# Attention with an infinite memory beside a Fourier filter: stack pieces in another order, chains of reciprocals a step sooner, last zeros all on GpSimd

## The chip, the cores and the metric

The kernel runs on one core of one Trainium2 chip. The metric is the device time of one execution in microseconds (us), the median of several runs.

## The reference

Two independent parts share the program. Part A is a causal multi-head attention of 32 heads of width 18 over 2048 tokens in four segments of 512, with a compressive memory that is carried from segment to segment; part B is a two-dimensional Fourier filter. Cut to what is computed:

```python
# A: x (1,2048,576), wq, wk, wv, wo (576,576), beta (32)
q, k, v = heads(x@wq), heads(x@wk), heads(x@wv)          # (1,32,4,512,18)
phi = lambda t: where(t > 0, t + 1, exp(t)); g = sigmoid(beta)
M = 0; z = 0
for s in range(4):
    p = softmax(qs @ ks^T * 18**-0.5 + causal_mask)
    a_dot = p @ vs
    a_mem = (phi(qs) @ M) / (phi(qs) @ z + 1e-6)
    outs.append(g * a_mem + (1 - g) * a_dot)
    M = M + phi(ks)^T @ vs;  z = z + sum(phi(ks))
a = merge_heads(outs) @ wo
# B: x (1,2048,576)
b = irfft2(rfft2(x) * (w_r + 1j*w_i))
return concatenate([a, b], axis=-1)
```

## The kernel before

The order of all work is written out by hand: each engine does its instructions in the order in which the program emits them. First come the Fourier part and the projections of part A (to about 357 us). Queries and keys go to DRAM as three bf16 parts each (`qkD`), values with a column of ones as `vD`. The change lies in what follows, `attention`.

**Steps and blocks.** The loop `for t in range(133)` in `attention` does one head of one segment a step: `k=t//4` counts groups of four heads, `hh=t%4` the head in the group, `n=t//8` blocks of eight heads, `g=t//32` segments. In step t the row maxima of head t+10 are found (`s1`), the scores of head t are computed and exponentiated (`s2`), and the products with the values of a group that is 5 to 8 steps older are accumulated (`pv`). TensorE takes them in that order, in pieces that alternate: `s1`, `s2`, `s1`, `s2`, `pv`, background, `s1`, `s2`. At the last head of a group (`hh==3`) the parts of P above the diagonal are set to zero by four instructions (`sel`, L697 to L699): before, on GpSimd, but for the groups k=29 to 31 the one of P0 by a minimum with a tile `cap` on VectorE. `cap` is built by GpSimd in steps 3 and 4 (L945, L946). `mpath` turns the maxima of a group into rows of the stack: VectorE, ScalarE and GpSimd (`mh`, L666 and L667), a transpose on TensorE (L670), a copy on ScalarE (`mts`, L673) and a small DMA on GpSimd's queue (L674).

**Stacks.** `s2` multiplies 108 rows: the 18 dimensions of a head six times, in combinations of the three bf16 parts. `stack_dmas(n,0)` returns the six DMAs that fill Q of block n, `stack_dmas(n,1)` those for K (L625; 144 KB and 18 partitions each). Q has three buffers, K four. `load_v(n)` (L632) loads the values of a block into `vs`, three buffers in turn. Before, at the first step of block n, Q of block n+2, K of block n+3 and `load_v(n+2)` are appended to a list `q`, of which two entries are issued a step, one at the start and one at the end. Q and K of a block are first read by `s1` ten steps ahead of its first head, that is in step 8n-2 for block n. All of these go through SP's queue, which issues in order and has at most eight DMAs on their way, since it uses eight semaphores in turn.

**Results of a block.** `pv_out` (L720) copies the sums to `U`, and five DMAs (`u_dmas`, L725 for the denominators `rD`, L730 for `uD`) store them, through a list `qu` of which two a step are issued.

**Chains of reciprocals.** `recip` loads 32 rows of denominators as `ry`, takes the reciprocal on VectorE (L740), scales it on ScalarE, splits it into three bf16 parts (L742 to L746), stores these (L748) and loads them again as 96 rows (L752). Each `yield` in it is a step; `slack` yields stand ahead of the store, two behind it. `rd` is the chain of the memory's denominators (`den`), `rr` that of the softmax, which starts eight steps into the next segment (`ln`), together with the first loads `ux` of the unscaled results. When it is through, `mixed(g)` is appended to the background list `bg`.

**Background.** `run_bg(1.2)` in the middle of a step and `run_bg(0)` at its end take one unit of the list each time 1.0 has been gathered: one a step, and two in every fifth. `mixed(g)` is a list of such units: `c` for `combine` (a product of TensorE that spreads the reciprocals over the rows, L819, in one bank of PSUM; a product on VectorE, L822 or L824; an addition, L825; a copy `oh` on ScalarE, L814, and a remainder `ol`, L809), `m` for the memory's part (L786 to L793) and `p` for the output projection (L856). Additions and remainders run on GpSimd until step 117, and on VectorE from then on. `pq_load` (L759) loads phi(q) for the memory's part, for the first segment that uses it in steps 16 to 20.

The functions that the diff touches, and what calls them:

Of the kernel before, what the change touches and what calls it, by code (L numbers as in the profile page):

```python
# [5 lines left out]
F32=mybir.dt.float32; F32R=mybir.dt.float32r  # L6
# [383 lines left out]
class ATT:  # L390
# [285 lines left out]
    def s2(s,t):  # L676
# [3 lines left out]
        P=s.P[k]  # L680
# [14 lines left out]
        if hh==3:  # L695
            def sel(x,pat):
                if k<29: nc.gpsimd.affine_select(out=x,in_=x,pattern=pat+[[1,128]],compare_op=OP.is_ge,fill=0.0,base=0,channel_multiplier=-1)  # L697
                elif x.tensor is not P[0].tensor: nc.gpsimd.affine_select(out=x,in_=x,pattern=pat+[[1,128]],compare_op=OP.is_ge,fill=0.0,base=0,channel_multiplier=-1)
                else: nc.vector.tensor_tensor(x,x,s.cap[:,None,:].to_broadcast([128,4,128]),op=OP.min)  # L699
            sel(P[0][:,:,:128],[[0,4]])  # L700
            sel(P[1][:,:,:128],[[0,4]])
            sel(P[1][:,:,384:],[[0,4]])
            sel(P[2][:,:,:128],[[0,4]])
# [17 lines left out]
    def u_dmas(s,n):  # L721
# [9 lines left out]
        return L  # L731
    def recip(s,src,dst,gate,eps,load,slack=0):
        nc=s.nc; tp=s.tp
# [14 lines left out]
        nc.sync.dma_start(bass.AP(tensor=dst.tensor,offset=dst.offset,ap=[[128,128],[32*512,3],[1,128]]),w)  # L748
        yield
        yield  # L750
        r=tp.tile([96,512],BF,name=load,bufs=1) if load!="re" else tp.tile([126,1024],BF,name="re",tag="pq",bufs=5)[:96,:512]
# [9 lines left out]
    def den(s,g,lane):  # L761
# [12 lines left out]
        def chain():  # L774
            yield
            yield
            yield
            yield from s.recip(s.dD[g],s.rdD[g],s.gt,True,"rd",2)
        lane.append(chain())
# [20 lines left out]
    def combine(s,g):  # L800

        nc=s.nc; tp=s.tp; xs=s.ux
        s.oh=[None]*5; s.ol=[None]*5
        eng=lambda: nc.vector if s.now>=117 else nc.gpsimd
        yield
        yield
        def low(u):
            r=126 if u<4 else 72
            eng().tensor_tensor(s.ol[u][:r],s.am[u][:r],s.oh[u][:r].bitcast(F32),op=OP.subtract)  # L809
        for t in range(7):  # L810
            if t>1:
                u=t-2; r=126 if u<4 else 72
                s.oh[u]=tp.tile([126,512],F32R,name="oh",bufs=5); s.ol[u]=tp.tile([126,512],F32R,name="ol",bufs=5)
                nc.scalar.copy(s.oh[u][:r],s.am[u][:r])  # L814
                if s.now<117: low(u)
            if t<5:
# [9 lines left out]
                if t<2: s.later(1,lambda t=t: s.ux_load(g,t+3))  # L826
            if t>1 and s.now>=117: low(t-2)
            yield
# [93 lines left out]
    def attention(s,tp,ps):  # L922
# [18 lines left out]
        lane=[]  # L941
        s.cap=tp.tile([128,128],F32,name="cap",bufs=1)
        for t in range(133):
            k,hh=divmod(t,4); n,qd=divmod(k,2); g=k//8
            if t==3: nc.gpsimd.memset(s.cap,3.0e38)  # L945
            if t==4: nc.gpsimd.affine_select(out=s.cap,in_=s.cap,pattern=[[1,128]],compare_op=OP.is_ge,fill=0.0,base=0,channel_multiplier=-1)  # L946
            if hh==0 and qd==0:
                if 0<n<14: q+=s.stack_dmas(n+2,0)
                if 0<n<13: q+=s.stack_dmas(n+3,1)
                if n+2<16: q.append(lambda n=n: s.load_v(n+2))  # L950
            st=t%32
            if 16<=t<21: s.pq_load(1,t-16)
            if t==34: bg.append(s.den(1,lane))
            if st==8 and g>0:
                def ln(g=g):
                    r=s.recip(s.rD[g-1],s.rrD[g-1],s.g1,False,"rr",2)
                    for i in range(8):
# [11 lines left out]
            b=s.s2(t) if t<128 else iter(())  # L969
            if q: q.pop(0)()  # L970
            if qu: qu.pop(0)()
# [23 lines left out]
            for l in list(lane):  # L995
                try: next(l)
                except StopIteration: lane.remove(l)
            if q: q.pop(0)()
            if qu: qu.pop(0)()
# [138 lines left out]
```

## Time and profile before

| | |
|---|---|
| median of 3 runs | 721.9 us (719.81 to 724.74) |
| the profiled execution | 723.57 us |
| its span, first to last instruction | 721.8 us |
| TensorE busy | 686.8 us, 95% |
| VectorE, ScalarE, GpSimd busy | 543.9, 449.0, 210.3 us |
| moved by DMA | 121.04 MB, 168 GB/s over the span |
| granted TensorE clock, mean | 0.997 |

In the profile, PE is TensorE's matmuls, PEld its weight loads, DVE VectorE, ACT ScalarE, POOL GpSimd and SP the engine that issues most DMAs; L697 is line 697 of the kernel. A group or row names the tiles as out<-in. Rows of the list of waits read: who <- whom, us in total, times, longest. Rows of a timeline read: start in us, length in us, engine, line, operation, tiles, form, count, and in brackets the idle time before it and what ended it. Rows of the chain read: start, length, what. A tile whose name is `x` in them is the stack's first buffer.

### The profile page before, as it was taken

The numbers are of one execution on the slowest core, as the hardware profiler recorded it, in microseconds if no ns is written. First come the engines' busy times: TensorE is split into PE (matmuls) and PEld (weight loads), VectorE is DVE, ScalarE is ACT, GpSimd is POOL, SyncE is SP. The second block draws the span as 40 slices with busy tenths as digits, with TensorE's granted clock in tenths as the row PEclk, the third lists the DMA queues.
The fourth block names the chain that finished last, engine by engine and source line by source line (L and its number), as shares of the span: only waits on it lengthen the run. The fifth ranks groups of instructions, "written<-read, shape, count | busy, mean of one in ns | idle before, by whom it ended". The sixth has DMA issues, their size and how long they took to land.

```text
span 721.8 us, 14187 instructions
## 1 busy us (share of the span) xinstructions
PE 686.8 (95%) x4879; PEld 496.2 (69%) x4879; DVE 543.9 (75%) x1215; ACT 449.0 (62%) x1012; POOL 210.3 (29%) x409
## 2 busy tenths in 40 slices
PE   4999999999999999999999899989999999998997
PEld 4999769879879789999744344434565445653587
DVE  5999989799789698887588778877566875666153
ACT  3657785585685564444488678767556775567631
POOL 2110000100100211565066344444233762427210
PEclk9999999999999999999999999999999999999999
DMA  9876436545373568889637666677556664431331
GB/s 322 268 231 214 144 120 200 178 167 178 135 240 121 159 219 271 202 239 216 186 96 178 163 170 149 174 170 168 141 128 176 166 162 128 124 100 43 97 99 65
DMA packets 83244, 121.04 MB, mean 168 GB/s; under 512 B 11352, under 2 KB 50630, under 8 KB 83036
## 3 DMA queue, kind: packets, MB, share of 16 engines
q1 hardware_dynamic: 76580, 104.11, 50.3%
q0 software_dynamic: 6592, 16.03, 7.8%
q8 instruction: 38, 0.62, 0.4%
q14 instruction: 34, 0.28, 0.1%
HBM read 81.78 MB, written 38.24 MB: 166 GB/s over the span
## 4 chain that ended last, share of the span: by engine, by line
PE 71%; DVE 9%; DMA 8%; ACT 6%; issue 4%; POOL 2%; SPq 0%; DVEq 0%; ACTq 0%
PE pj L464 12%; PE pv L714 10%; PE po L856 7%; PE pjv L464 7%; PE s L641 5%; PE s L649 3%; PE s L684 3%; DMA yb<-yout 3%; PE i L300 3%; PE i L311 3%; PE s L688 2%; DMA Qs<-qkD 2%; PE po L886 2%; PE pn L786 2%; PE c L163 2%
## 5 line engine op out<-in xcount | busy, mean ns | idle before, releaser
L645 DVE CUSTOM_DVE_ANT_0 junk<-s,mask 128x512 bf16<-128x512 f32 (+1 forms) x256 | 141.3, 552 | 58.5 <-PE s L641 53.3
L651 DVE TENSOR_REDUCE mx<-s 128x4 f32<-128x512 f32 x128 | 87.9, 687 | 13.7 <-PE s L650 10.8
L714 PE MATMUL pv<-P,vs 128*32 128x512 f32 (+3 forms) x1024 | 89.1, 444 | 1.1 <-DVE P L699 0.4
L685 ACT ACTIVATE P<-s 128x512 f32<-128x512 f32 x128 | 77.5, 605 | 18.0 <-PE s L684 14.3
L694 ACT ACTIVATE P<-s 128x256 f32<-128x256 f32 x128 | 49.9, 390 | 50.6 <-PE s L693 50.5
L690 ACT ACTIVATE P<-s 128x512 f32<-128x512 f32 x128 | 77.4, 604 | 0.0
L697 POOL TENSOR_SCALAR_AFFINE_SELECT P<-P 128x512 f32<-128x512 f32 x116 | 69.8, 637 | 6.1 <-ACT P L694 3.2
L464 PE MATMUL pj<-x,wqkh 128*128 128x512 f32 x162 | 56.4, 409 | 0.0
L511 POOL MEMSET vt<- 128x32 f32 x16 | 2.4, 161 | 151.8 <-PE pm L521 124.1
L210 DVE TENSOR_TENSOR t<-Z 128x580 f32<-128x580 f32 x64 | 46.2, 757 | 0.1
L210 DVE TENSOR_TENSOR Z<-t 128x580 f32<-128x580 f32 x64 | 45.8, 756 | 0.1
L641 PE MATMUL s<-Ks,Qs 108*128 108x512 bf16 (+1 forms) x128 | 42.2, 330 | 0.0
L142 PE MATMUL f<-ftab,eh 128*128 128x290 f32 (+1 forms) x160 | 31.2, 313 | 9.8 <-ACT eh L126 8.9
L300 PE MATMUL i<-civ,Y 128*128 128x256 f32 (+1 forms) x288 | 37.8, 284 | 0.8 <-DVE T L332 0.8
L714 PEld LDWEIGHTS pv<-P,vs 128*32 128x32 f32 x1024 | 22.3, 108 | 22.6 <-issue 15.4
L311 PE MATMUL i<-itab,T 128*128 128x290 f32 (+1 forms) x224 | 36.4, 311 | 0.2 <-DVE yout L319 0.2
L300 PEld LDWEIGHTS i<-civ,Y 128*128 128x128 f32 (+1 forms) x288 | 35.7, 181 | 1.0 <-DVE T L332 1.0
L464 PEld LDWEIGHTS pj<-x,wqkh 128*128 128x128 f32 x162 | 30.4, 188 | 7.7 <-issue 1.0
L464 PE MATMUL pj<-xh,wqkh 128*128 128x512 f32 x90 | 35.6, 396 | 0.0
L464 PE MATMUL pj<-x,wqkl 128*128 128x512 f32 x90 | 35.5, 395 | 0.0
L464 PE MATMUL pj<-xh,wqkl 128*128 128x512 f32 x90 | 35.5, 394 | 0.0
L650 PE MATMUL s<-tri,idb 128*128 128x256 bf16 x128 | 34.9, 273 | 0.0
(213 smaller groups left out, 1819.6 us busy)
## 6 DMA issues: line engine op xcount, KB each, us to landing
qkD<-sp SPq DMA_DIRECT2D x36, 384.0 KB
Ks<-qkD SPq DMA_DIRECT2D x72, 144.0 KB
x<-qkD SPq DMA_DIRECT2D x60, 144.0 KB
Qs<-qkD SPq DMA_DIRECT2D x60, 144.0 KB
xin<-xb SPq DMA_DIRECT2D x16, 384.0 KB
cfw<-cfw POOLq DMA_DIRECT2D x16, 384.0 KB, 4.3
civ<-civ POOLq DMA_DIRECT2D x16, 384.0 KB, 7.4
vs<-vD SPq DMA_DIRECT2D x16, 330.0 KB
```

The source lines that it names most:

```text
L210: v.tensor_tensor(o,a,b,op=op)
L300: nc.tensor.matmul(p[:m,k],Y[i][:,q,c*128:c*128+m],cc[:,hl,o:o+256],start=n==0,stop=n==5)
L311: nc.tensor.matmul(p,x,t,start=n==0,stop=n==6)
L464: s.nc.tensor.matmul(out,a,b,start=i==0,stop=i==len(L)-1)
L641: nc.tensor.matmul(out,Q[:108,h,128*i:128*i+128],K[:108,h,:128*(i+1)],start=True,stop=True)
L645: nc.vector.tensor_tensor_reduce(out=junk[:,:w],in0=src,in1=s.mask[:,512-w:],scale=1.0,scalar=-3.0e38, op0=OP.add,op1=OP.max,accum_out=s.m ...
L651: nc.vector.tensor_reduce(out=s.mx[k][:,hh],in_=pa.rearrange("p (b c) -> p b c",c=128),axis=mybir.AxisListType.X,op=OP.max)
L685: nc.scalar.activation(P[0][:,hh],p0,AF.Exp,scale=SC)
L690: nc.scalar.activation(P[1][:,hh],p1,AF.Exp,scale=SC)
L697: if k<29: nc.gpsimd.affine_select(out=x,in_=x,pattern=pat+[[1,128]],compare_op=OP.is_ge,fill=0.0,base=0,channel_multiplier=-1)
L714: nc.tensor.matmul(s.pvt[32*hh:32*hh+32,128*j:],vt[:,j,19*h:19*h+32],mv[0][:,hh,mv[1]],start=j==0,stop=j==2,skip_group_check=True)
L856: nc.tensor.matmul(ps,a[t][:r,c],b[:r,t,w],start=i==0,stop=i==14)
```

## The change

Four things are done.

- **Stacks.** In the first step of a block (`r8==0`) the six DMAs of Q are appended, and in this step three entries of `q` are issued at its start and three at its end; in every other step one, at its start. `load_v` is appended a step later, the six DMAs of K another step later. The first segment's `pq_load` moves from steps 16 to 20 to steps 19 to 23.
- **Chains of reciprocals.** `recip` takes the number of yields between its store and its load as `gap`. The chains `rr` and `rd` go from `slack` 2 and two yields to `slack` 1 and three; `rr` starts at the seventh step of a segment and not at the eighth.
- **Zeros.** All four `sel` of every group run on GpSimd; `cap` is gone.
- **Remainders.** The remainders `ol` of the last `combine` run on VectorE from step 110 on, and are held back until step 118 has been passed; its additions stay where they were.

```diff
@@ s2
             def sel(x,pat):
-                if k<29: nc.gpsimd.affine_select(out=x,in_=x,pattern=pat+[[1,128]],compare_op=OP.is_ge,fill=0.0,base=0,channel_multiplier=-1)
-                elif x.tensor is not P[0].tensor: nc.gpsimd.affine_select(out=x,in_=x,pattern=pat+[[1,128]],compare_op=OP.is_ge,fill=0.0,base=0,channel_multiplier=-1)
-                else: nc.vector.tensor_tensor(x,x,s.cap[:,None,:].to_broadcast([128,4,128]),op=OP.min)
+                nc.gpsimd.affine_select(out=x,in_=x,pattern=pat+[[1,128]],compare_op=OP.is_ge,fill=0.0,base=0,channel_multiplier=-1)
@@ recip
-    def recip(s,src,dst,gate,eps,load,slack=0):
+    def recip(s,src,dst,gate,eps,load,slack=0,gap=2):
...
         nc.sync.dma_start(bass.AP(tensor=dst.tensor,offset=dst.offset,ap=[[128,128],[32*512,3],[1,128]]),w)
-        yield
-        yield
+        for _ in range(gap): yield
@@ den
-            yield from s.recip(s.dD[g],s.rdD[g],s.gt,True,"rd",2)
+            yield from s.recip(s.dD[g],s.rdD[g],s.gt,True,"rd",1,3)
@@ combine
-        s.oh=[None]*5; s.ol=[None]*5
+        s.oh=[None]*5; s.ol=[None]*5; lows=[]
         eng=lambda: nc.vector if s.now>=117 else nc.gpsimd
...
-            eng().tensor_tensor(s.ol[u][:r],s.am[u][:r],s.oh[u][:r].bitcast(F32),op=OP.subtract)
+            (nc.vector if s.now>=110 else nc.gpsimd).tensor_tensor(s.ol[u][:r],s.am[u][:r],s.oh[u][:r].bitcast(F32),op=OP.subtract)
...
-                if s.now<117: low(u)
+                if s.now<110: low(u)
...
-            if t>1 and s.now>=117: low(t-2)
+            if t>1 and s.now>=110: lows.append(t-2)
+            if s.now>=118:
+                while lows: low(lows.pop(0))
             yield
@@ attention
-        s.cap=tp.tile([128,128],F32,name="cap",bufs=1)
         for t in range(133):
             k,hh=divmod(t,4); n,qd=divmod(k,2); g=k//8
-            if t==3: nc.gpsimd.memset(s.cap,3.0e38)
-            if t==4: nc.gpsimd.affine_select(out=s.cap,in_=s.cap,pattern=[[1,128]],compare_op=OP.is_ge,fill=0.0,base=0,channel_multiplier=-1)
-            if hh==0 and qd==0:
-                if 0<n<14: q+=s.stack_dmas(n+2,0)
-                if 0<n<13: q+=s.stack_dmas(n+3,1)
-                if n+2<16: q.append(lambda n=n: s.load_v(n+2))
+            r8=t%8
+            if r8==0 and 0<n<14: q+=s.stack_dmas(n+2,0)
+            if r8==1 and n+2<16: q.append(lambda n=n: s.load_v(n+2))
+            if r8==2 and 0<n<13: q+=s.stack_dmas(n+3,1)
             st=t%32
-            if 16<=t<21: s.pq_load(1,t-16)
+            if 19<=t<24: s.pq_load(1,t-19)
             if t==34: bg.append(s.den(1,lane))
-            if st==8 and g>0:
+            if st==7 and g>0:
                 def ln(g=g):
-                    r=s.recip(s.rD[g-1],s.rrD[g-1],s.g1,False,"rr",2)
+                    r=s.recip(s.rD[g-1],s.rrD[g-1],s.g1,False,"rr",1,3)
...
-            if q: q.pop(0)()
+            for _ in range(3 if r8==0 else 1):
+                if q: q.pop(0)()
...
-            if q: q.pop(0)()
+            for _ in range(3 if r8==0 else 0):
+                if q: q.pop(0)()
```

## The prediction

> **What bounds the kernel now.** I read the page first: the span and the busy line, which say that TensorE (PE) is the bound over the whole span.
>
> ```profile
> span 721.8 us, 14187 instructions
> PE 686.8 (95%) x4879; PEld 496.2 (69%) x4879; DVE 543.9 (75%) x1215; ACT 449.0 (62%) x1012; POOL 210.3 (29%) x409
> ```
>
> The reader sees 95% on PE: a change that removes no matmul can only win what PE stands idle. Everything in the diff lies in the attention loop, from about 357 us to the end, so the second view is the list of PE's waits in that stretch.
>
> ```profile
> PE s L649 <- DMA Ks<-qkD: 3.1, 1, 3.1
> PE s L649 <- DVE mx L651: 2.1, 5, 1.0
> PE mt L670 <- POOL mh L667: 1.9, 2, 1.5
> PE s L649 <- DMA Qs<-qkD: 1.6, 1, 1.6
> ...
> PE s L684 <- ACT P L685: 0.9, 2, 0.7
> ...
> PE s L649 <- DVE mg L663: 0.5, 1, 0.5
> ...
> PE pb L819 <- DMA rr<-rrD: 0.4, 1, 0.4
> PE pv L714 <- DVE P L699: 0.4, 1, 0.4
> ```
>
> Four things that the diff touches can be won: two waits for stack pieces (3.1 and 1.6), one for a chain of reciprocals (0.4), and the knot in which GpSimd (POOL) delivers `mh` late and VectorE the last zeros (1.5, 0.7, 0.4). That is 7.7 us, 1.1% of the span, if all of it goes and nothing comes in its place. About 1% is also what a measurement of this kernel can tell from no change.
>
> Third, the transfers: windows of the loop, with share of the 16 DMA engines and GB/s as the last two figures.
>
> ```profile
> 373.00:377.00 4.00, 4.00 (x33) 1.43 (x31) 3.50 (x12) 3.49 (x9) 2.45 (x5) 1.00 0.63 143
> 380.00:384.00 4.00, 4.00 (x33) 1.86 (x34) 3.71 (x13) 3.38 (x10) 3.60 (x7) 1.00 0.64 147
> 425.00:431.00 6.00, 6.00 (x58) 2.59 (x60) 4.64 (x15) 4.36 (x12) 0.75 (x3) 1.00 0.61 153
> 433.00:436.00 3.00, 3.00 (x22) 1.16 (x20) 2.86 (x8) 2.86 (x7) 0.73 (x2) 1.00 0.30 80
> 463.00:465.00 2.00, 2.00 (x26) 1.19 (x26) 1.64 (x6) 1.45 (x5) 0.57 (x1) 1.00 0.16 46
> ...
> 665.00:721.80 56.80, 51.84 (x373) 40.17 (x373) 18.01 (x28) 21.34 (x48) 6.38 (x12) 0.98 0.25 83
> ```
>
> Where stack pieces make up most of what moves, the share stands at 0.61 to 0.64 and the rate near 150 GB/s, in windows 50 us apart. That looks like a ceiling, not like a queue short of work: a piece of 144 KB (147.5 kB) then costs 1.0 us of the queue and the twelve of a block 12 us. The rows of 433 and 463 are the slack: 3.0 us at 0.30 and 2.0 us at 0.16 instead of 0.63, that is 1.6 and 1.5 us of transfer time not used.
>
> The Trainium skill, page "DMA: Bandwidth & Descriptors", section "Why a DMA increments its semaphore by 16 and not by 1", has a transfer use the largest number of engines up to 16 that divides its outer dimension; for the 18 partitions of a piece that would be 9 of 16, 0.56, near the measured 0.61 to 0.64. The same page's section "Bandwidth" gives 341 GB/s for 1 MB from 128 partitions; six pieces would then land in an estimated 2.6 us instead of 6, and the first rival below would hold. By the first of the two sections the trace agrees with the ceiling, by the second it doesn't.
>
> **The change, part by part.** *The stack pieces.* Steps are counted by the first matmul of `s2`, L684, one a step. Per block n the six Q pieces are now all issued in step 8n, `load_v` in 8n+1, K pieces one a step from 8n+2; before, two DMAs went out per step: Q, K, then `load_v`. No DMA is added; the order on SP's queue changes, and the five `pq` loads go from steps 16-20 to 19-23.
>
> ```profile
> 371.28 1.84 SPq L625 DMA_DIRECT2D x<-qkD  x5
> ...
> 378.08 0.86 PE L714 MATMUL pv<-P,vs 128*32 128x128 f32 x16
> ...
> 387.35 0.38 PE L684 MATMUL s<-Qs,Ks 110*128 110x512 bf16 x1
> ...
> 394.24 0.86 PE L714 MATMUL pv<-P,vs 128*32 128x128 f32 x16
> ...
> 402.16 0.38 PE L649 MATMUL s<-x,Qs 108*128 108x384 bf16 x2 [3.09 <-DMA Ks<-qkD]
> ...
> 418.60 0.39 PE s L649 x2
> ```
>
> The first of these rows are the timelines of SP and PE, the last is one of the chain. Between the two L714 rows, the third `pv` of blocks 1 and 2, lie 16.2 us; in a block the queue has its 12 us of pieces, a `vs` and five `U` stores to move, so it is nearly the bound by itself, and with the `pq` loads more than that. Step 16 starts at 387.35. Its Q pieces (block 4) are wanted at step 22, where PE waits 3.09 us until 402.16. With all six issued in step 16 and no `pq` between them they land about 2 us after the K pieces ahead of them, six pieces later: 387.4 + 4 for the backlog + 6 = 397.5, before 399.1. The 3.1 us go there. But the next deadline is Q of block 5, for L649 at 418.60 (step 30). Ahead of it in the queue stand the same bytes as before: Q3, K4, Q4, K5, two `vs`, the `pq` loads, eight `uD` stores. A full queue delivers the same sum at the same time, so PE, which would now be there at 418.6 - 3.1 - 0.5 = 415.0 (the 0.5 is the wait put down to L663, which ends at this L649), waits again.
>
> There is also a new wait. `vs` has three buffers, so `load_v` for block n+2 needs the last `pv` of block n-1, which PE does in step 8n+3. It is now issued in 8n+1 and holds SP: in block 1 until 378.94 (first L714 row), where six Q pieces from 371.28 on are issued by 373.5. Behind it on SP stand an `ob` load and all K pieces; nobody waits for those within four steps. The price is a hole in a full queue.
>
> ```profile
> 459.52 0.38 SPq L748 DMA_DIRECT2D rrD<-rw  x1
> ...
> 463.77 0.32 SPq L752 DMA_DIRECT2D rr<-rrD  x1
> 464.14 1.90 SPq L625 DMA_DIRECT2D Qs<-qkD  x5
> ...
> 465.83 0.38 PE L819 MATMUL pb<-rr,sel 96*126 96x512 bf16 x1 [0.42 <-DMA rr<-rrD]
> ...
> 472.27 0.38 PE L649 MATMUL s<-x,Qs 108*128 108x384 bf16 x2 [1.56 <-DMA Qs<-qkD]
> ```
>
> From an empty queue a load lands 2.1 us after its issue (463.77 to 465.83). So block 1's pieces land from 373.4 to 378.5 and the next transfer at 381.1 instead of 379.5: a hole of 1.6 us. In block 2 SP is held until 395.1, but 4 + 6 us of transfers cover it: no hole. Bounds for this part up to step 30: -3.6 (no wait left at 418.60) to +1.6 (the same bytes plus the hole). The full-queue rows are nearer: I take **-0.5**.
>
> *The reciprocal chains.* `rr` starts a step sooner and its store is issued two steps sooner, its load one; for `rd` only the store moves. No instruction is added. Before, SP, which issues in order, stood before the load until the store had landed at 463.77, with five Q pieces behind it; that made the hole of 1.5 us at 463 and then 0.42 + 1.56 us of wait on PE. Now the loads stand three steps behind (about 6 us against 4.25 from store to load). So Q of block 8 lands up to 1.5 us sooner: 470.7. The hole of 1.6 from block 1 is swallowed by the slack at 433. PE, 0.5 sooner, wants it at 472.27 - 1.98 - 0.5 = 469.8 and still waits 0.9. So step 54 comes 1.5 us sooner in all: **-1.0** for this part (bounds -2.0, all of the wait, and +1.0, if `load_v` of block 5, held until step 43, delays the stores).
>
> ```profile
> 446.92 0.95 DVE L740 RECIPROCAL ry<-ry 128x128 f32<-128x128 f32 x1
> ...
> 449.51 0.95 DVE L740 RECIPROCAL ry<-ry 128x128 f32<-128x128 f32 x1
> ...
> 451.06 0.38 PE L649 MATMUL s<-Ks,x 108*128 108x384 bf16 x2 [1.03 <-DVE mx L651]
> ```
>
> The two reciprocals, a step apart, fall into the same step (42). VectorE does the same sum before step 45's L649, so the 1.03 us stay: 0 (bounds -1.0 and +1.0). `mixed` starts a step sooner for all groups; for g=1 and 2 its adds and subtractions meet GpSimd's selects at other steps: 0 (bounds -0.5 and +0.8).
>
> *The knot at steps 115 to 121.*
>
> ```profile
> 649.52 0.61 POOL L674 DMA_DIRECT2D x<-mts  x1 [1.83 <-ACT mts L673]
> 650.14 2.39 POOL L697 TENSOR_SCALAR_AFFINE_SELECT P<-P 128x512 f32<-128x512 f32 x4
> 651.10 0.68 DVE L824 TENSOR_TENSOR ux<-ux,pb 126x512 f32<-126x512 f32 x1
> 652.50 2.51 POOL L825 TENSOR_TENSOR am<-ux,am 126x512 f32<-126x512 f32 x2
> 654.98 1.28 POOL L809 TENSOR_TENSOR ol<-am,oh 126x512 fp32r<-126x512 f32 x1
> 656.23 1.25 POOL L825 TENSOR_TENSOR am<-ux,am 126x512 f32<-126x512 f32 x1
> 657.44 0.19 POOL L666 CAST mh<-mg 128x16 bf16<-128x16 f32 x1
> 657.70 0.68 POOL L667 TENSOR_TENSOR mh<-mg,mh 128x16 bf16<-128x16 f32 x1
> 660.01 0.39 ACT oh L814
> 660.09 4.06 POOL L698 TENSOR_SCALAR_AFFINE_SELECT P<-P 128x512 f32<-128x512 f32 x3 [0.18 <-ACT P L690]
> ```
>
> GpSimd is busy without a break from 649.52 to 658.4, and PE's transpose L670 waits 1.5 us for it. Taking the `ol` (1.28) away looks like a gain. But `combine` runs a step sooner, so four of its adds instead of three fall before step 118 and stay on GpSimd: 4 x 1.25 against 3 x 1.25 + 1.28, the same. And the first add is now issued in step 115 ahead of that step's four selects; it needs VectorE's product, ready some 0.3 sooner than 651.8, while GpSimd was free for selects at 650.14. So: 651.5 + 5.0 + 2.4 + 0.9 for `mh` = 659.8, against 658.4: +1.4. Behind it ScalarE has one copy of `oh` (0.4) fewer in its row before the next `pv`. The zeros of P0 move from VectorE, whose last one PE waited 0.4 us for, to GpSimd, where they come first of four. With the `ol` on VectorE beside them a select takes up to 4.06/3 = 1.35 us instead of 0.6, still before the `pv` that reads it, which comes after two more steps of ScalarE. 1.4 - 0.4 - 0.4: I take **+0.6** for the knot (bounds -2.6, all its waits gone, and +3.0, twice the wait for `mh`).
>
> The Trainium skill, page "SBUF — State Buffer", section "Who interferes with whom", says that a VectorE instruction with two SBUF inputs contends with a GpSimd one that reads SBUF; the row of 1.35 us a select agrees. By that rule the last zeros all on GpSimd cost an estimated 4 x 1.35 = 5.4 us in a row beside the burst, not 2.4; `pv` takes them over three steps.
>
> The rest is hidden. Building `cap` is two small instructions on GpSimd in steps 3 and 4, for which nobody in the list of waits waits. The zeros of k=30 and 31 fall behind 665 us, where GpSimd is busy 6.4 of 56.8 us; without that cover two selects of 0.6 would stand ahead of a `pv`, 1.2 us.
>
> Sum: -0.5 - 1.0 + 0 + 0.6 = **-0.9 us**. The profiled execution is 723.57 (span 721.8 and 1.8 around it): 722.7 after. It lies 1.7 above the median of the runs shown, 721.9; on that scale **721.0**.
>
> **The rivals.** *The queue has room.* If the ceiling is only the order of issue, Q comes early every time: -3.6 - 2.0, and with the knot eased by half, -1.3, it is -6.9: 715. For it: the waits on DMA are named in the list, and the Q pieces do go first. Against: the share of 0.61 to 0.64 in every window. With all 2.6 of the knot it would be 713.7.
>
> *`load_v` starves the queue* (slower). Place: SP, steps 8n+1 to 8n+3. Price: the hole of 1.6 us in each of the blocks 1 to 5, 8.0 us, less the 1.6 of slack at 433, and the knot's 0.6: +7.0, 728.9. It decides as soon as the six Q pieces have landed before the third `pv` of the block, that is where less than 1 us of older transfers is queued at step 8n. For it: block 1 does just that. Against: block 2 has 4 us queued, and the rows are full until 431.
>
> *The knot tightens.* `mh` later by 3 us and ScalarE's row behind it: +3.0 with -1.5 from the loads: 723.4.
>
> *It doesn't do what it says.* SP, held by `load_v` until step 43, reaches the stores so late that the loads stand close behind them again: -0.5 + 0.6: 722.0.
>
> **How the numbers follow.** Forecast, within 3 us of 721.0: 0.50. Doesn't do what it says: 0.10. Queue has room: 0.18. Starved queue: 0.14. Tighter knot: 0.08. The range must take most of the second and third: 715 to 728 leaves out about 0.08 below and 0.09 above. Faster by over 1% (under 714.7) needs the room and all of the knot, 0.12; slower by over 1% (over 729.1) the starved queue in every block, 0.13; within 1%, 0.75.
>
> **What would show it.** Right: no wait on DMA at step 22, but one of 2 to 4 us at step 30; SP's L632 waiting 3 to 6 us for `pv` in every block; no hole near 463 and SP's load of `rr` without a wait; the share still 0.61 to 0.64; GpSimd's first L825 ahead of four selects, and L670 waiting 2 to 3 us. Wrong: no wait at step 30 (the queue had room), or windows of a share under 0.3 at each block's second step (starved), or L670 without a wait, or waits at places that this account doesn't name.

## The result and the profile after

The changed kernel takes **726.21 us** (median of 20 runs, 721.01 to 732.30) against 722.88 us before (20 runs, 719.37 to 727.22): ratio 1.0045, 95% interval 1.0025 to 1.0065. The ratios here and below leave out a run that is over 1.5% above the fastest of its kernel: the one of 732.30 us (the median of the other 19 is 725.68) and one of 733.68 us of stacks and tail. The change makes the kernel slower by 3.3 us; the forecast was 0.9 us faster, and its range took the measured time in. The interval reaches 0.2% to either side; the prediction took about 1% for what a measurement can tell from no change. The profiled execution took 722.63 us and is thus one of the shorter ones of its kernel. That matters below: its mean granted clock is 0.997, as in the profile of before, while the 20 runs have 0.9938 on the mean.

The page of after, first lines:

```profile
span 720.9 us, 14173 instructions
PE 686.9 (95%) x4879; PEld 495.2 (69%) x4879; DVE 541.1 (75%) x1212; ACT 449.9 (62%) x1012; POOL 210.8 (29%) x410
```

TensorE does the same work. The list of PE's waits in the loop of after (who <- whom, us in total, times, longest):

```profile
PE s L649 <- DMA Qs<-qkD: 3.1, 1, 3.1
...
PE mt L670 <- POOL mh L667: 2.0, 2, 1.6
...
PE pb L816 <- DMA rr<-rrD: 1.4, 1, 1.4
PE po L855 <- ACT oh L811: 1.1, 1, 1.1
```

The 3.1 us for `Ks` at step 22 are gone and 3.1 us for `Qs` are there, at step 30; the 1.6 us at step 53 are gone, and the 0.4 us for `rr` have become 1.4. Where the time went is read from the start of single steps (L684), first in the timeline of before, then in that of after, for steps 0, 22, 32, 54, 114 and 122:

```profile
355.69 0.38 PE L684 MATMUL s<-x 110*128 110x512 bf16 x1
...
402.49 0.38 PE L684 MATMUL s<-Qs,Ks 110*128 110x512 bf16 x1
...
423.20 0.38 PE L684 MATMUL s<-Qs,x 110*128 110x512 bf16 x1
...
472.60 0.38 PE L684 MATMUL s<-x,Ks 110*128 110x512 bf16 x1
...
646.74 0.38 PE L684 MATMUL s<-Qs,Ks 110*128 110x512 bf16 x1
...
666.95 0.38 PE L684 MATMUL s<-x,Ks 110*128 110x512 bf16 x1
```

And of after:

```profile
353.59 0.38 PE L684 MATMUL s<-x 110*128 110x512 bf16 x1
...
397.14 0.38 PE L684 MATMUL s<-Qs,Ks 110*128 110x512 bf16 x1
...
421.98 0.38 PE L684 MATMUL s<-Qs,x 110*128 110x512 bf16 x1
...
471.68 0.38 PE L684 MATMUL s<-x,Ks 110*128 110x512 bf16 x1
...
645.93 0.38 PE L684 MATMUL s<-Qs,Ks 110*128 110x512 bf16 x1
...
666.36 0.38 PE L684 MATMUL s<-x,Ks 110*128 110x512 bf16 x1
```

The loop begins 2.10 us sooner in after; what lies ahead of it is a part of the program that the change doesn't touch, so that is taken off. By stretches, after less before (last column: the profile of the same changed kernel in a second comparison, below):

| steps | before, us | after, us | difference | second profile |
|---|---|---|---|---|
| 0 to 22 | 46.80 | 43.55 | -3.25 | -3.24 |
| 22 to 32 | 20.71 | 24.84 | +4.13 | +2.24 |
| 32 to 54 | 49.40 | 49.70 | +0.30 | +0.71 |
| 54 to 114 | 174.14 | 174.25 | +0.11 | +0.83 |
| 114 to 122 | 20.21 | 20.43 | +0.22 | +0.23 |
| 122 to the end | 54.89 | 54.56 | -0.33 | -0.33 |
| sum | | | +1.18 | +0.44 |

Two things make this table too kind to the change. Both profiles of the changed kernel are of short executions (722.63 us, and 722.98, the shortest of 12), so what the median run lost beyond them isn't in it. And before lost 1.7 us of clock in steps 114 to 122 (shown below), which hides as much in that row.

In the windows of after (share of the DMA engines and GB/s last, the granted clock ahead of them) the stretch of the second row shows two things:

```profile
374.00:378.00 4.00, 4.00 (x44) 1.92 (x36) 3.15 (x10) 3.33 (x9) 1.92 (x5) 1.00 0.59 119
...
410.00:414.00 4.00, 2.77 (x21) 0.96 (x18) 2.95 (x11) 2.75 (x8) 1.25 (x4) 1.00 0.86 161
414.00:418.00 4.00, 2.14 (x11) 0.95 (x15) 1.03 (x2) 0.60 (x2) 0.00 (x0) 0.71 0.63 150
418.00:422.00 4.00, 4.00 (x40) 1.76 (x41) 2.36 (x8) 2.35 (x6) 1.49 (x3) 0.86 0.57 184
```

The queue works on while PE waits (161 and 150 GB/s), and after the wait the clock stands at 0.71 and 0.86: 4 x 0.29 + 4 x 0.14 = 1.7 us of matmul time lost. In the second profile of the changed kernel the clock doesn't fall there, and this row is 1.9 smaller. So the wait has a second price, and it is not paid each time.

### The profile page after: what moved, and what is told of

Its sections match the earlier page's. It is cut to its first block, busy times and chain, and to the rows that moved or that the text cites. A ratio compares the mean times of both kernels' runs of the same rounds, so it can differ in the third digit from the quotient of the medians.

```text
span 720.9 us, 14173 instructions
## 1 busy us (share of the span) xinstructions
PE 686.9 (95%) x4879; PEld 495.2 (69%) x4879; DVE 541.1 (75%) x1212; ACT 449.9 (62%) x1012; POOL 210.8 (29%) x410
## 4 chain that ended last, share of the span: by engine, by line
PE 70%; DMA 12%; DVE 8%; ACT 5%; issue 3%; POOL 1%; SPq 0%; ACTq 0%; DVEq 0%; POOLq 0%
PE pj L464 12%; PE pv L712 10%; PE pjv L464 8%; PE po L855 7%; PE s L641 5%; PE s L649 3%; PE s L684 3%; DMA Qs<-qkD 3%; PE s L688 2%; PE po L885 2%; DMA vs<-vD 2%; PE pn L783 2%; PE i L300 2%; PE c L163 2%; PE pm L521 2%
## 5 line engine op out<-in xcount | busy, mean ns | idle before, releaser
L697 POOL TENSOR_SCALAR_AFFINE_SELECT P<-P 128x512 f32<-128x512 f32 x128 | 79.3, 653 | 22.4 <-ACT P L685 15.8
```

## The experiments

All comparisons are with the kernel before on the same chip. The last two columns are from the profile and from the records of all runs: what PE waited for DMA from step 16 to 67, and the mean granted clock (before: 0.9959 over the 144 runs of these comparisons, 0.9953 to 0.9965 in single ones).

| kernel | median, us | before, us | ratio (95%) | waits for DMA, us | clock |
|---|---|---|---|---|---|
| the change, again | 727.17 | 722.73 | 1.0056 (1.0024 to 1.0087) | 4.2 | 0.9930 |
| stacks alone | 727.93 | 722.73 | 1.0075 (1.0051 to 1.0100) | 7.7 | 0.9924 |
| chains alone | 726.26 | 722.73 | 1.0052 (1.0028 to 1.0075) | 4.1 | 0.9928 |
| zeros and remainders alone ("tail") | 720.05 | 722.73 | 0.9972 (0.9946 to 0.9998) | 4.2 | 0.9962 |
| change, `pq` loads later | 725.60 | 721.68 | 1.0060 (1.0036 to 1.0084) | 6.6 | 0.9939 |
| change, matmuls in the wait | 724.32 | 721.68 | 1.0050 (1.0025 to 1.0074) | 3.4 | 0.9958 |
| change, `load_v` later | 725.36 | 721.68 | 1.0047 (1.0017 to 1.0076) | 5.4 | 0.9951 |
| change, both later | 724.93 | 721.68 | 1.0046 (1.0024 to 1.0069) | 3.6 | 0.9950 |
| chains and tail | 723.25 | 723.40 | 0.9998 (0.9975 to 1.0021) | 6.2 | 0.9958 |
| stacks and tail | 726.91 | 723.40 | 1.0052 (1.0022 to 1.0082) | 10.4 | 0.9919 |
| change, `combine` at its old step | 726.28 | 723.40 | 1.0051 (1.0027 to 1.0074) | 8.6 | 0.9933 |
| tail, `pq` loads later | 719.08 | 723.40 | 0.9947 (0.9923 to 0.9970) | 5.0 | 0.9961 |
| change, fewer bytes | 722.99 | 722.16 | 1.0007 (0.9982 to 1.0033) | 3.7 | 0.9952 |
| before, fewer bytes | 718.88 | 722.16 | 0.9952 (0.9931 to 0.9973) | 1.7 | 0.9970 |
| tail, `pq` later, chains, `combine` old | 719.17 | 721.52 | 0.9959 (0.9935 to 0.9983) | 1.8 | 0.9967 |

Before itself has 5.1 us in the fifth column (3.1 + 1.6 + 0.4). In the tail alone 2.0 us of it, at the place of the wait for `Ks`, and in the last row all of it are put down to "issue" by the profile. Each kernel has one profile, and waits differ from one execution to the next: that at step 22, in code that the edits up to there hardly touch, was 3.1 us in before, 2.9 in chains alone, 2.5 in chains and tail and 2.0 in the tail alone. A difference of 1 us between two rows of that column shows nothing by itself.

### The change again, and its three parts alone

The changed kernel without an edit, and the kernel before with one part each: the stack pieces with `load_v` and the `pq` loads; the two chains; the zeros with the remainders.

```diff
 e_stacks
-            if hh==0 and qd==0:
-                if 0<n<14: q+=s.stack_dmas(n+2,0)
-                if 0<n<13: q+=s.stack_dmas(n+3,1)
-                if n+2<16: q.append(lambda n=n: s.load_v(n+2))
+            r8=t%8
+            if r8==0 and 0<n<14: q+=s.stack_dmas(n+2,0)
+            if r8==1 and n+2<16: q.append(lambda n=n: s.load_v(n+2))
+            if r8==2 and 0<n<13: q+=s.stack_dmas(n+3,1)
...
 e_chains
-            if st==8 and g>0:
+            if st==7 and g>0:
...
-                    r=s.recip(s.rD[g-1],s.rrD[g-1],s.g1,False,"rr",2)
+                    r=s.recip(s.rD[g-1],s.rrD[g-1],s.g1,False,"rr",1,3)
...
 e_tail
-                if k<29: nc.gpsimd.affine_select(...)
-                elif x.tensor is not P[0].tensor: nc.gpsimd.affine_select(...)
-                else: nc.vector.tensor_tensor(...)
+                nc.gpsimd.affine_select(...)
...
-            if t>1 and s.now>=117: low(t-2)
+            if t>1 and s.now>=110: lows.append(t-2)
+            if s.now>=118:
+                while lows: low(lows.pop(0))
```

> The changed kernel once more, beside the kernel before. Theory G (the clock): the idle time of TensorE is the same in both, and what is lost is TensorE's clock, which falls for some us after the wait of 3.1 us that now stands at step 30; so runs of this kernel differ as their mean granted clock does, by 7.2 us for each 0.01, from about 719 at 0.999 to 728 at 0.987, and the kernel before has the higher clock on average (0.995 to 0.997 against 0.993). Theory S (the sum of waits): the loss of 3.3 us lies in waits that are new (for rr at step 50, for copies of ScalarE at 85 and 120), and the clock of both kernels is the same on average.

> The kernel before with only the new order of stack pieces, load_v and pq loads. Both theories: the wait at step 22 is gone and one of 3 us stands at step 30. Theory G: slower by 1.5 to 3.5 us with a clock lower by 0.002 to 0.004, since the wait at step 30 lets the clock fall more often than that at step 22 did. Theory S: within 1 us of the kernel before, since the wait has only moved and the new waits belong to the other parts.

> The kernel before with only the chains of reciprocals a step sooner. Theory G: 0 to 1.5 us faster; SP does not stand before the load of rr, and the wait for Q at step 54 shrinks from 1.6 to under 1. Theory S: 1 to 2 us slower, with a wait of over 1 us for rr or for copies of ScalarE, since mixed comes a step sooner and meets other work.

> The kernel before with only the zeros on GpSimd and the remainders on VectorE. combine is not a step sooner here, so GpSimd has three additions and no remainder ahead of mh: the wait of L670 falls from 1.5 to 0.3 us. Theory G: 1 to 3 us faster, since the clock does not fall at step 121 either. Theory S: faster by no more than the wait that goes, 1.2 us.

The stack pieces cost 0.75%, the chains 0.52%, and the tail wins 0.28%. Theory G's lower clock came in the change and in the stacks, and its 1 to 3 us for the tail (2.7 by the medians). But it had the stacks too cheap (5.2 us by the medians, not 1.5 to 3.5) and the chains as a gain, where 3.5 us were lost; theory S's 1 to 2 us for the chains are too few as well. The loss of the stacks alone is seen in the waits; first in the list of e_stacks:

```profile
PE pb L819 <- DMA rr<-rrD: 3.8, 1, 3.8
PE s L649 <- DMA Qs<-qkD: 2.8, 1, 2.8
```

The wait of step 22 came back at step 30, as forecast, and the one for `rr`, 0.4 us before, grew to 3.8 us.

The loss of the chains alone lies mainly in the knot, at step 118, fifteen steps behind the start of the last segment's chain (step 103). The timeline of GpSimd in e_chains:

```profile
655.51 1.26 POOL L824 TENSOR_TENSOR am<-ux,am 126x512 f32<-126x512 f32 x1
656.75 1.27 POOL L808 TENSOR_TENSOR ol<-am,oh 126x512 fp32r<-126x512 f32 x1
657.98 1.26 POOL L824 TENSOR_TENSOR am<-ux,am 126x512 f32<-126x512 f32 x1
659.20 1.26 POOL L808 TENSOR_TENSOR ol<-am,oh 126x512 fp32r<-126x512 f32 x1
660.43 2.31 POOL L824 TENSOR_TENSOR am<-ux,am 126x512 f32<-126x512 f32 x1
...
662.95 0.22 POOL L667 TENSOR_TENSOR mh<-mg,mh 128x16 bf16<-128x16 f32 x1
```

With `combine` a step sooner, two remainders and four additions stand ahead of `mh`; PE waited 5.1 us for it at L670, and the clock was low from the end of that wait on. The windows of e_chains behind the waits of 2.9 us (step 22) and 5.1 us:

```profile
399.00:407.00 8.00, 7.10 (x43) 2.93 (x44) 3.22 (x8) 2.91 (x6) 1.56 (x3) 0.57 0.68 172
...
656.00:672.00 16.00, 10.46 (x60) 4.74 (x58) 6.21 (x12) 8.43 (x19) 10.41 (x11) 0.69 0.11 31
```

That is 8 x 0.43 = 3.4 us and 16 x 0.31 = 5.0 us lost. But step 22 is the same code as in before, where the wait was longer (3.09 us) and the clock stayed at 1.00. This part of that profile is thus no loss of the chains.

### The parts in pairs

> The kernel before with the chains a step sooner and with the zeros on GpSimd and the remainders on VectorE, but the old order of the stack pieces. Theory K (the chains alone lost their time in the knot, where two remainders and four adds stood on GpSimd ahead of mh and TensorE waited 5.1 us; the tail takes the remainders away): the chains' loss goes, but so does most of the tail's gain, because the first add still stands ahead of the four zeros: 722 to 723 us, ratio 0.999 to 1.002, L670 waiting about 1.6 us for mh instead of 5.1, and a wait of 1.2 to 1.6 us for rr at step 50. Theory A (the parts add up, each with its own loss): 1.0052 and 0.9972 together, 1.0024, 724 us. Step 22 keeps its wait for Ks of 2 to 3 us in both.

> The kernel before with the new order of the stack pieces and with the zeros and remainders of the tail, but the old chains. Theory D (the queue is full from step 16 to step 52 and a wait that one load loses comes back at the next): no wait at step 22, 2.7 to 3.1 us at step 30 for Qs, 3 to 4 us at step 51 for rr, whose store and load are still behind one another; the tail's gain of 2.9 us at the end stays whole: 1.0075 and 0.9972 together, ratio 1.0045 to 1.005, 725 to 726 us. Theory O (only the order of issue counts, and the loss of the stack pieces alone came from the clock): at most 1.002, 723.5 us.

The edits are those above, two at a time. Chains and tail together are level with before (0.9998): the tail takes the remainders away from GpSimd, L670 waits 1.6 us instead of 5.1, and the tail's own gain is used up. That is theory K, as far as this profile shows; `rr` waited 3.1 us, not the 1.2 to 1.6 that it named. The ratios alone hardly tell K from A: the sum of the two parts, 1.0024, lies outside the interval, if only just, and has an uncertainty of its own. Stacks and tail are slower by 0.52%, near the 0.45 to 0.5% of theory D, with 3.1 us at step 30 and this one row from the list of e_stail at step 51:

```profile
PE pb L817 <- DMA rr<-rrD: 5.8, 1, 5.8
```

So the stack pieces are what makes the change slower: the ratio rises by 0.0075 when they are put on before, by 0.0080 on the tail, and by 0.0047 to 0.0058 on chains and tail.

### What in the new order costs

Four edits of the changed kernel: the `pq` loads behind the Q pieces of step 24; twelve matmuls of 512 columns, whose result nobody reads, ahead of `s1` in step 30, so that PE is busy where it waited; `load_v` at step 8n+4; and the first and the third together.

```diff
 e_pqlate
-            if 19<=t<24: s.pq_load(1,t-19)
...
+            if t==24:
+                for i in range(5): s.pq_load(1,i)
 e_fill
+            if t==30:
+                f=s.ps.tile([128,512],F32,name="fill",tag="post")
+                for _ in range(12): nc.tensor.matmul(f,s.Ks[n%4][:108,0,:128],s.Ks[n%4][:108,0],start=True,stop=True)
 e_loadv
-            if r8==1 and n+2<16: q.append(lambda n=n: s.load_v(n+2))
+            if r8==4 and n+2<16: q.insert(0,lambda n=n: s.load_v(n+2))
```

> The changed kernel with the five pq loads behind the Q pieces of block 5 (step 24) instead of ahead of them. If the sum of bytes ahead of Q sets step 30, 1.2 MB less takes 4 to 5 us from it: the wait of 3.1 us at step 30 is gone. Theory G: faster than the changed kernel by the wait and the clock that falls behind it, 3.5 to 5.5 us (2 us faster than the kernel before), mean clock 0.996 or more. Theory S: faster by the wait alone, 2.5 to 3.1 us, with the clock unchanged. If the order within the queue does not matter: no change.

> The changed kernel with twelve matmuls of 512 columns on data that is there (2.6 us of TensorE, results read by nobody) ahead of the scores of step 30, so that TensorE works where it waited. Theory G: the clock does not fall there, the mean clock rises by 0.002 or more and the kernel is 1 to 3 us faster than the changed one, though it does more work. Theory S: the same time within 0.5 us, or slower by up to 2.6 us in runs in which the wait was shorter.

> The changed kernel with load_v in step 8n+4 instead of 8n+1, behind the last read of its buffer, so that SP does not stand before it. The hole in the queue at 375 to 377 us goes, so Q of block 5 comes 1.0 to 1.6 us sooner: the wait at step 30 falls from 3.1 to 1.5 to 2.1 us. Theory G: 1.5 to 3 us faster, since a shorter wait lets the clock fall less often. Theory S: 1.0 to 1.6 us faster. If SP's wait costs nothing: no change.

> The changed kernel with both: pq loads behind Q of block 5, load_v in step 8n+4. No wait on a transfer up to step 50. Theory G: 4 to 6 us faster than the changed kernel, 1 to 3 faster than the kernel before, clock 0.997. Theory S: 3 us faster than the changed kernel, level with the kernel before.

None gives the loss back, where both theories had forecast gains; all intervals overlap that of the change. With the `pq` loads later the wait at step 30 went, and 1.7 us for `dD` at step 37, 1.2 us for `vs` at step 45 and 3.7 us for `rr` at step 50 were there. With `load_v` later the wait at step 30 was 4.4 us and not 1.5 to 2.1, so SP held by `load_v` isn't its cause. With both, 1.4 us at step 37 and 1.6 us at step 45 came in. The matmuls bear on the part of the clock: the mean of the runs rose to 0.9958 (before has 0.9965 in this comparison), the wait at step 30 shrank to 1.3 us, and that for `rr` grew to 2.1. The kernel was still 2.6 us above before by the medians, 3.6 by the ratio. Of these the matmuls themselves explain 1.2 (step 29 to 30 takes 6.4 us, against 5.3 in the second profile of the change, which lost no clock there) and the clock about 0.0007 x 721 = 0.5; what the other 0.9 to 1.9 are isn't shown.

### Bytes or order

> The changed kernel with one yield more between the end of the chain and the start of mixed, den and oproj, so that combine runs at its old step and only the loads of rr come sooner. Theory K (the gain of the tail is lost because combine moved, and rr's wait at step 50 is there because its reader moved with it): the wait for rr at step 50 goes (1.4 us), the first add on GpSimd stands behind the four zeros again, L670 waits 0.7 us instead of 1.6, and the clock loses nothing there; 2.5 to 4 us less than the changed kernel, 722 to 723.5 us, ratio to before 1.000 to 1.002. Theory D alone (the queue's bytes): the rr wait goes or shrinks, but Qs of block 8 waits for as much at step 53; only the knot is won, 1 to 2 us, 724.5 us.

> The kernel before with the zeros and remainders of the tail, and the five pq loads moved from steps 16 to 20 to steps 25 to 29, behind the pieces of block 1's and 2's stacks and into the stretch before the queue's slack at step 36. Theory D (the pq loads' 1.1 MB are what the wait at step 22 pays for, and there are 3 us of slack at steps 36 and 50 to pay them from): no wait at step 22, at most 1.5 us at step 30, the slack at step 36 filled; 2 to 3 us less than the tail alone, 717 to 718 us, ratio 0.993 to 0.995. Rival (the full queue gives every wait back, as with the pq loads moved in the changed kernel): 720 us, 0.997, with the wait found at steps 30, 45 or 51.

> The changed kernel with the pq loads of group 1 cut to 128 of 512 columns (the other 384 are set to 1.0 on GpSimd, so the loads move 0.29 instead of 1.15 MB; the output of group 1's memory part is another). Theory D (the queue's bytes set the waits): 0.86 MB at 171 GB/s are 5 us of transfer; no wait at step 30, none for rr at step 50, and the clock loses nothing there: 5 to 6 us less than the changed kernel, 720 us, ratio 0.994 to 0.998, and level with the kernel before cut in the same way within 1 us. Theory O (the order is late by itself): the wait for Qs at step 30 stays at 2 us or more, or comes back at steps 45 to 53; 724 us, ratio 1.002 or more, and 3 us above the kernel before cut in the same way.

> The kernel before with the same cut of the pq loads of group 1. Theory D: no wait for Ks at step 22; the waits at steps 51 and 53 stay, since the store of rr and its load stand behind one another with the queue empty; 3 to 3.5 us less than before, ratio 0.995 to 0.996. Theory O: the same here, since only the new order differs; what tells them apart is the distance between the two kernels, under 1 us by D, 3 us or more by O.

```diff
 e_combold
                     yield from r
+                    yield
                     bg.append(s.mixed(g))
 e_tailpq (tail with)
-            if 16<=t<21: s.pq_load(1,t-16)
+            if 25<=t<30: s.pq_load(1,t-25)
 e_lite_after, e_lite_before
-        s.nc.sync.dma_start(x[:r],s.pqD[g][126*t:126*t+r])
+        c=128 if g==1 else 512
+        if g==1: s.nc.gpsimd.memset(x[:,c:],1.0)
+        s.nc.sync.dma_start(x[:r,:c],s.pqD[g][126*t:126*t+r,:c])
```

`combine` at its old step mended what theory K said, 0.4 us for `rr` and 0.7 us at L670. But the waits turned up elsewhere, 4.6 us at step 30, 2.3 us for `vs` at step 53 and 1.3 us for `pq` at step 66, and the time is unchanged (1.0051). Theory K's 2.5 to 4 us were won at the knot alone (steps 114 to 122 take 17.3 us instead of 20.4) and lost again; D had the waits come back, though at step 53 and with 1 to 2 us left over. With the `pq` loads later in the old order there is no wait at step 22, and with the tail the kernel takes 0.53% less than before. The tail alone wins 0.28% of that; the intervals of the two overlap, so what the loads add isn't shown by the times.

The fewer bytes decide between D and O, and not as D expected. Both kernels gain about 3 us by them (before 3.3, from 722.16 to 718.88; the change 2.7 to 3.5, from a ratio of 1.0045 or 1.0056 to 1.0007, times 722), and both lose their first wait almost whole (0.7 us left at step 30, none at step 22). But the distance between the two stays, 722.99 - 718.88 = 4.1 us, where D expected under 1 and O 3 or more. So bytes set the waits at steps 22 and 30, and the loss of the changed kernel lies elsewhere too: at the knot, which these bytes don't reach, and at the load of `rr`. SP's rows and PE's for `rr` in e_lite_after:

```profile
458.31 0.42 SPq L749 DMA_DIRECT2D rr<-rrD  x1
...
463.41 0.59 PE L818 MATMUL pb<-rr,sel 96*126 96x512 bf16 x1 [3.04 <-DMA rr<-rrD]
```

and in e_lite_before:

```profile
458.05 0.31 SPq L752 DMA_DIRECT2D rr<-rrD  x1
...
460.45 0.43 PE L821 MATMUL pb<-rr,sel 96*126 96x512 bf16 x1
```

Issued at the same time, the load takes 5.1 us in the one, with PE waiting 3.0, and at most 2.4 in the other, with no wait. The windows around it, first of e_lite_after, then of e_lite_before:

```profile
458.00:460.00 2.00, 2.00 (x18) 0.83 (x17) 1.81 (x8) 1.56 (x4) 0.42 (x2) 1.00 0.79 223
...
458.00:460.00 2.00, 2.00 (x30) 1.16 (x26) 1.64 (x6) 1.45 (x5) 0.46 (x1) 1.00 0.30 72
```

In e_lite_before SP stands before this load until its store has landed, the queue runs low (72 GB/s), and the load has it nearly to itself. In e_lite_after K pieces and stores are issued until just ahead of it (223 GB/s), and it lands behind them. Either part of the change does this alone: from its issue to its reader the load has 6.0 us in e_stacks (461.41 to 467.40) and 5.7 us in e_ctail (459.17 to 464.89), with waits of 3.8 and 3.1 us. After the wait in e_lite_after the clock lost 10 x 0.34 = 3.4 us more, by its window:

```profile
460.00:470.00 10.00, 6.96 (x37) 3.22 (x38) 4.26 (x11) 3.01 (x7) 3.10 (x5) 0.66 0.65 154
```

### The chains with their reader in place

```diff
 e_best (e_tailpq with e_chains and)
                     yield from r
+                    yield
                     bg.append(s.mixed(g))
```

> The version with the zeros and remainders of the tail, the old order of the stack pieces and the pq loads at steps 25 to 29, and with it the chains a step sooner, but combine at its old step. Theory F (the load of rr needs 5 us from issue to landing in a full queue instead of 2.0 from an empty one; a step more of lead pays for that, and what is won is the queue's time that was lost ahead of it): no wait for rr (0.8 us in the version without the chains), less than 1 us for Qs at step 53 instead of 1.9, the knot as in the tail alone (L670 0.7 us): 1.5 to 2.5 us less, 717 us, ratio 0.992. Rival (the queue is full and pays later): the wait for Qs at step 53 stays, or pq waits 1 us at step 66; 719 to 720 us, ratio 0.995 to 0.996.

SP's and PE's rows for `rr` in e_best:

```profile
457.06 0.43 SPq L749 DMA_DIRECT2D rr<-rrD  x1
...
464.81 0.43 PE L816 MATMUL pb<-rr,sel 96*126 96x512 bf16 x1
```

The load has 7.7 us, and neither `rr` nor Q of block 8 is waited for. From step 50 to 55 the profile shows 11.9 us, against 14.1 in before and 16.3 in e_tailpq, 1.7 of the latter lost by the clock: the local gain that theory F expects, at the place where it expects it. The time of all runs doesn't show it (0.9959 against 0.9947 for e_tailpq, intervals overlap): theory F's 717 us was missed, and 719.17 lies where its rival put it. In this profile a wait of 1.8 us at step 45, with 1.7 us of clock, takes part of it back, at neither of the two places that the rival named. Three versions beat both kernels: e_tailpq by 0.53%, e_best by 0.41% and e_tail by 0.28%; the three intervals overlap.

## Why the prediction was wrong

**The stack pieces (-0.5).** Right in its steps: no wait at step 22 (-3.25 with what lies around it), Q of block 5 waits again at step 30, 3.1 us where 2 to 4 were named. SP's rows in after:

```profile
369.18 2.23 SPq L625 DMA_DIRECT2D x<-qkD  x6
376.90 0.39 SPq L632 DMA_DIRECT2D vs<-vD  x1
...
452.62 0.38 SPq L746 DMA_DIRECT2D rrD<-rw  x1
...
458.96 0.42 SPq L749 DMA_DIRECT2D rr<-rrD  x1
459.56 3.49 SPq L625 DMA_DIRECT2D Qs<-qkD  x6
466.01 0.38 SPq L632 DMA_DIRECT2D vs<-vD  x1
```

`load_v` does hold SP, from 371.4 to 376.9 in block 1. By the two profiles the part comes to +0.9 and -1.0 up to step 32 (the first two rows of the table together); most of the difference is the clock after the wait, 1.7 us, a term that the sum didn't have. At equal clock the part is -0.8 and -1.0, near the forecast. But the term ended at step 30. Put on chains and tail, the pieces cost the runs 3.4 to 4.2 us (0.0047 to 0.0058 times 722); about 0.0021 x 721 = 1.5 of these go with the clock, and where the rest lies isn't shown. Nor is the ceiling of about 150 GB/s one of the whole queue: in the rows of 410 and 418 above it moved 161 and 184.

**The chains (-1.0): the step that failed.** "No hole near 463" and "`rr` load without a wait of SP" are right, as the rows of 452.62 to 459.56 show. Q of block 8 came in time, better than forecast. But the wait for `rr`, 0.42 us that the sum took as gone, became 1.4 us, and the part comes to +0.3 and +0.7 (steps 32 to 54). The prediction gave this load no time to land in a full queue; the only landing time that it had, 2.1 us, it had itself read as that of an empty queue. Measured: 463.80 - 458.96 = 4.8 us. And it counted the load a step sooner without the load's reader, which `ln` appends behind it and which moved along.

**`mixed` sooner (0).** +0.11 and +0.83, inside the bounds but for 0.03 us; a wait of 1.1 us for ScalarE's `am` at step 85 is new in both profiles.

**The knot (+0.6): too small.** The order was right to the instruction. GpSimd in after:

```profile
650.87 1.26 POOL L822 TENSOR_TENSOR am<-ux,am 126x512 f32<-126x512 f32 x1 [1.54 <-DVE ux L821]
652.09 2.39 POOL L697 TENSOR_SCALAR_AFFINE_SELECT P<-P 128x512 f32<-128x512 f32 x4
654.45 3.72 POOL L822 TENSOR_TENSOR am<-ux,am 126x512 f32<-126x512 f32 x3
...
658.39 0.22 POOL L667 TENSOR_TENSOR mh<-mg,mh 128x16 bf16<-128x16 f32 x1
```

L670 waited 1.6 us, less than the 2 to 3 named, and the stretch gave +0.22. But that is measured against a stretch in which before's profile lost clock, 12 x 0.14 = 1.7 us, by its window:

```profile
656.00:668.00 12.00, 9.16 (x67) 4.17 (x59) 6.55 (x12) 8.11 (x20) 6.97 (x8) 0.86 0.13 40
```

In e_lite_before, which has before's code here and lost no clock in it, steps 114 to 122 take 18.65 us, so the 20.43 of after are +1.8, with the work that the earlier `combine` brings into these steps. About 1.0 of it are waits: those over 0.3 us sum to 3.7 us in after and to 2.7 in e_lite_before. The largest that no term of the sum has is that of 1.1 us at L855 for ScalarE's copy `oh`, where the prediction took 0.4 off for one copy fewer. The tail alone takes 17.3 us for these steps, 2.9 less than before (about 1.6 of it clock), and so does e_combold: `combine` a step sooner costs the change 3.1 us here.

**The rivals.** The queue had no room: a wait stood at step 30. The starved queue, the slower case, came near in time (728.9) and not in mechanism: with `load_v` later nothing changed. That the range took the measured time in is luck, since its upper end was set for this case. The knot didn't tighten in the change; in e_chains it did, by 3.6 us of wait. The change did what it said: the loads no longer stood close behind the stores.

**What the sum lacked.** It had no term for the clock. At a mean of 0.9937 (31 runs of the changed kernel) instead of 0.9959, an estimated 0.0022 x 721 = 1.6 us are lost. The waits come on top: at equal clock the two profiles give +1.2, where both lost 1.7, and 0.4 + 1.7 = 2.1, where the second lost none in the loop. Together that is 2.8 to 3.7 us, beside 3.3 measured. So the chains failed in sign, the knot came to as much as three times its term, and the clock stood in none. That is the account of two short executions. The parts put on one another over all runs show the largest miss at the stack pieces, 3.4 to 4.2 us in place of -0.5; no trace of a long execution of the changed kernel shows how the two fit, so that stays open. The part of the clock is worked out from the runs' records; in which step the runs that have no trace lose it isn't shown.

## What to carry to other kernels

A load's time from issue to landing belongs to the queue as it stood then: who fills a hole in a queue takes the short time away from the load that stood behind the hole. When a chain is moved ahead, look whether its reader moves with it, and when a wait on a full queue is removed, look for the next loads, here at steps 30, 45, 50, 53 and 66. Put a part of a change on its own, and in pairs: here one part won 0.28%, one lost 0.75%, and one lost 0.52% alone and half of that beside the first.

## What the runs showed of the hardware

The clock is lost in equal pieces. Behind a wait of 2.0 us at step 22 of e_tail:

```profile
398.00:406.00 8.00, 5.99 (x44) 2.67 (x45) 3.62 (x12) 3.24 (x8) 2.00 (x5) 0.79 0.66 168
```

and around the wait of 2.7 us in the second profile of the changed kernel:

```profile
414.00:421.00 7.00, 4.41 (x44) 2.22 (x45) 3.41 (x12) 3.07 (x8) 1.69 (x5) 1.00 0.59 159
```

8 x 0.21 = 1.7 us there, none here; 1.7 at step 30 of after, 3.4 and 5.0 in e_chains, each near one, two or three times 1.7. In windows of 1 us the clock of e_tail reads 0.50 from 402 to 404, so a piece is some 3.4 us at half the clock. The Trainium skill, page "TensorE: Matmul & The Clock Gate", section "What's actually happening", has a free-running window of 3413 ns, and TensorE at half its clock after an idle one. Half of 3.4 us is 1.7 us, an estimate from that page, and the trace agrees with this size. It doesn't agree with the idle window, which only the waits of 3.7 us or more could fill. In the 17 profiles all six waits of 3.7 us or more were followed by such a loss, and 7 of the 12 between 2.0 and 3.1 us; so were single waits of 1.7 to 1.9 us in e_lite_before, e_best and e_tailpq. The Trainium skill, same page, section "Why this matters for your kernels", asks for no gap above about 3 us. Here 1.8 us were enough in one execution (e_best), and 3.1 us were harmless in another (before).
